# Pooled keys and values of the first two batches summed on TensorE in float32, their weights turned there, and a new decode of the layer weights

## The chip, the cores and the metric

The kernel runs on one core of one Trainium2 chip. The metric is device time in microseconds (us) of one execution, from three executions. "Span" is the time from the first to the last instruction of the profiled execution.

## What is computed

An attention with pooled keys and values feeds two layers, the first with a rational function inside, the second with a squared rectifier.

```python
def _attn_ref(q, k, v):                       # (8, 8, 576, 64) each, pool = 8
    k_p = k.reshape(B, H, Sp, pool, D).mean(axis=3)
    v_p = v.reshape(B, H, Sp, pool, D).mean(axis=3)
    scores = scale * np.matmul(q, k_p.transpose(0, 1, 3, 2))
    attn = np.exp(scores - np.max(scores, axis=-1, keepdims=True))
    attn = attn / (np.sum(attn, axis=-1, keepdims=True) + 1e-09)
    return np.matmul(attn, v_p)

def _moe_ref(x, w_in, w_out, a, b):           # x: 4608 x 512, w_in: 512 x 2048
    h = x @ w_in
    P = a[0] + a[1] * h + a[2] * h**2 + a[3] * h**3
    Q = 1.0 + np.abs(b[0]) * np.abs(h) + np.abs(b[1]) * h**2
    return (P / (Q + 1e-6)) @ w_out

def _moe2_ref(x, w_in, w_out):
    h = np.maximum(x @ w_in, 0.0)
    return h * h @ w_out
```

The weights are float64; q, k and v are float32, and q and k are large (some 33 times a tenth of a normal draw), so that the scores need the accuracy of float32.

## The kernel before

**Work and tiles.** The 4608 tokens are nine blocks of 512, and these stand in four groups (`SBS`: two, two, two and three blocks). Each group goes through four phases: phases 0 and 1 are the halves of the first layer's 2048 hidden columns, phases 2 and 3 those of the second. A phase is eight f-tiles of 128 columns for each block of the group; one f-tile of one block is a slot. The first group so has 64 slots, numbered 0 to 63; phases 0 and 1 are slots 0 to 31. A slot has `mm1` (12 matmuls of 128x512 into `h`), VectorE's and ScalarE's work on `h` (`first`, `second`), and `mm2` (12 matmuls into four `y` tiles). Both products take three passes over a high and a low float32r half. In phases 0 and 1 VectorE has six operations of 512 a slot, in 2 and 3 one.

**Attention.** A chunk is 128 tokens of all eight heads, four chunks a block. `qk` gives the scores, `row_max` and `exps` the exponentials, `norm` divides, `a_split` (L696) makes two fp16 tiles of 128 columns a head of them and has the DMA transpose them (`turn`, SP's queue), `av` (L711) multiplies with the split values, `x_out` makes the layer's input `x`. The first nine chunks (`NF`) take q and pooled k in float32, the others bf16 parts. Block 0 needs chunks 0 to 3, block 1 chunks 4 to 7; a batch is 4.5 chunks, so these use batches 0 and 1.

**Pooling.** Batch 0's k and v come in whole (`k_first`, `v_first`) and VectorE sums them over eight tokens; for all others the first of eight slices is loaded and seven are added to it by DMAs that POOL issues, one after the other (`k_add`, `v_add`). `v_split` makes three bf16 parts, with four small copies by DMA.

**Weights.** An f-tile's weights are 1 MB of float64 words. `w_raw` loads them into one of three buffers (`ya`, `yb`, `wraw`); `w_decode` (L486) takes the exponent on ScalarE (a copy scaled by 2^-112), moves the low word's bits (VectorE, or ScalarE in phase 1), joins them on VectorE (`stt`), joins the sign in a second `stt`, and makes the high and low halves. For the twelve f-tiles in `BY_DMA` (2 to 7 of phases 0 and 1) the second `stt` writes a tile `t` and frees the raw buffer; ScalarE writes the high half and the negated low one, and a DMA of POOL adds `t` to the latter. Each f-tile is then stored for the later groups.

**Order.** A planner (`Plan`) takes all instructions down with an estimate of their cost and gives out the program order of every engine by list schedules. SP and POOL issue DMAs in that order; some are tied to an instruction of another engine, so that they start no earlier than planned (`_holds`).

Of the kernel before, what the change touches and what calls it, by code (L numbers as in the profile page):

```python
# [34 lines left out]
LN_SHIFT = 60  # L35
A_SHIFT = 15
# [10 lines left out]
BY_DMA = {(ph, f) for ph in (0, 1) for f in range(2, FH)}  # L47


class View:  # L50
    """Part of a planned tile: what will be taken from the real one when it exists."""
# [28 lines left out]
    def apart(self, other):  # L80
        """Whether two views of a tile surely share nothing: where they part, they take slices
        of the same thing that do not meet."""
        for a, b in zip(self.chain, other.chain):
            if a == b:
                continue
            if a[0] != "__getitem__" or b[0] != "__getitem__":
                return False
            for i, j in zip(a[1][0], b[1][0]):
                (i0, i1), (j0, j1) = (
                    (x, x + 1) if isinstance(x, int) else (x.start or 0, x.stop or 1 << 30)  # L90
                    for x in (i, j)
                )
# [25 lines left out]
class Plan:  # L118
    """Takes down the kernel's instructions in the order of their meaning, with about what they
    take, and gives them out in an order that keeps the engines busy. The order comes from list  # L120
    schedules forwards (the most urgent of what is ready first) and backwards (as late as the
    engines allow, which is what says how urgent an instruction is)."""
# [249 lines left out]
def fused_kernel(  # L372
# [4 lines left out]
    kf: bass.AP,  # L377
# [77 lines left out]
    sh_bias = const.tile([128, 1], F32, "sh_bias")  # L455
    a_1 = const.tile([128, H, 128], F16, "a_1")
    a_2 = const.tile([128, H, 128], F16, "a_2")

    def setup():
# [3 lines left out]
        plan.add("dve", 0.07, [(fill, dict(out=a_2[:, :, KC:128], x=0.0))])  # L463

# [10 lines left out]
    def w_raw(ph, f, tag):  # L475
        """Words of an f-tile's part of w_in and of w_out."""
# [9 lines left out]
    def w_decode(ph, f):  # L486
        """2^-112 takes 7 * 128 off the exponent field of the high word seen as a float32:
        its 11 bits then hold a float32's exponent, 3 bits too low. On ScalarE, the low word's upper
        half u becomes its top 3 bits by rounding u / 8192 less almost a half."""
# [3 lines left out]
        act(n, AF.Copy, out=f32(g), in_=f32(g), scale=2.0 ** -112)  # L493
# [27 lines left out]
    xt = {}  # L521
    kst, vst, kp_t, vp_t = {}, {}, {}, {}
    q_in, q_t, e_t, sm_t, at_t, x_ps = {}, {}, {}, {}, {}, {}

    def k_add(b, r):
        if b == 1:
            shape, src = [128, H // 2, SP], kf[b, :, r].rearrange("p (g k) -> p g k", g=4)
        else:
            shape, src = [128, H, SP], kt[b - 2, :, r]
        n = 128 * shape[1] * SP * 4  # L530
        if r == 0:
            kp_t[b] = p1.tile(shape, F32, f"kp{min(b, 2)}")
# [4 lines left out]
    def v_add(b, r):  # L537
        n = SP * DM * 4
        if r == 0:
            vp_t[b] = p1.tile([SP, DM], F32, "vp")  # L540
            load(n, vp_t[b], vt[b, :, r], SUM_EARLY)
        else:
            load_add(n, vp_t[b], vt[b, :, r], SUM_EARLY)

    def k_first():
        """Batch 0's k, in room that the blocks' x takes later."""
        t = px.tile([128, 2, 4, TB], F32, "x").rearrange("p a b c -> p (a b c)")
        n = 4 * SP
        raw = t[:, 0:POOL * n].rearrange("p (r k) -> p r k", r=POOL)
        load(128 * POOL * n * 4, raw, kf[0])  # L550
        kp = t[:, POOL * n:(POOL + 1) * n].rearrange("p (g k) -> p g k", g=4)
        dve(
            POOL * n, "tensor_reduce",
            out=kp, in_=raw.rearrange("p r (g k) -> p g k r", g=4), axis=AX.X, op=ALU.add,
        )
        kp_t[0] = kp

    def v_first():
        t = px.tile([128, 2, 4, TB], F32, "x").rearrange("p a b c -> p (a b) c")[0:SP]
        load(SP * DM * POOL * 4, t, vt[0])  # L560
        vp_t[0] = p1.tile([SP, DM], F32, "vp")
        for i in range(2):
            d = slice(i * DM // 2, (i + 1) * DM // 2)
            dve(
                POOL * DM // 2, "tensor_reduce",
                out=vp_t[0][:, d], in_=t[:, :, d].rearrange("p r d -> p d r"), axis=AX.X, op=ALU.add,
            )

    def k_split(b):
# [3 lines left out]
        act(n, AF.Copy, out=k[0], in_=kp)  # L573
        tt(n, kp, kp, k[0], ALU.subtract)
# [19 lines left out]
    def q_first():  # L594
        """The first chunks' q, in room that weights take later."""
# [42 lines left out]
    def qk(c, half):  # L638
        """Scores of the even or of the odd heads: in what follows, head 2g + a is at a, g."""
# [3 lines left out]
        else:  # L643
            ps = ps_s.tile([128, H // 2, SP], F32, "sc")
# [18 lines left out]
        pe((0.95 if c < NF else 0.4) * len(list(runs(c))), mm)  # L663
        sc_t[c, half] = ps

    def row_max(c, half):
# [6 lines left out]
        dve(H // 2 * SP, "tensor_reduce", out=mx, in_=sc_t[c, half], axis=AX.X, op=ALU.max)  # L673
# [311 lines left out]
```

## Time and profile before

| | us |
|---|---|
| three executions | 1761.91, 1768.87, 1783.73 |
| their median | 1768.87 |
| span of the profiled execution | 1782.6 |
| that execution's own time | 1783.73 (the one of the three that can hold this span) |

The profiled execution is so the longest of the three, 14.9 us above the median. In it PE is busy for 94% of the span, DVE for 65%, ACT for 63%, POOL for 6%. A busy share is a mean over stages with different limits, so the first 420 us are read by stretches. "PE" are matmuls, "PEld" their weight loads, "SPq" SP's queue; an idle time in brackets names what ended it.

### The profile page before, as it was taken

The page shows a single profiled execution, that of the slowest core. Times are in us where ns is not written, and L with a number is a line of the kernel's source. Part 1 is how long each engine was busy: PE and PEld are TensorE (multiplying, and loading weights), DVE is VectorE, ACT ScalarE, POOL GpSimd, SP SyncE. Part 2 cuts the span into 40 slices and gives each one's busy share as a digit, 9 for nine tenths or more (in the row PEclk, how much of TensorE's full clock was granted, in tenths as well). Part 3 has the DMA queues.
Part 4 walks back from the last instruction along what each step waited for, and adds up shares of the span by engine and source line. Part 5 has one row for each costly group of instructions (what it writes and reads, how often), then busy time and mean ns, then how long its engine had stood idle before and what let it go on. Part 6 is the DMA issues. An engine that isn't in the chain of part 4 may idle for free.

```text
span 1782.6 us, 23502 instructions
## 1 busy us (share of the span) xinstructions
PE 1677.6 (94%) x8752; PEld 1369.3 (77%) x8752; DVE 1166.6 (65%) x1886; ACT 1129.2 (63%) x2336; POOL 98.2 (6%) x115
## 2 busy tenths in 40 slices
PE   2269899899999999999999999999999999999999
PEld 2148777687788888888888888888888888888887
DVE  7459999867569898344588994444988999211112
ACT  4467877678766666666666686766766666433332
POOL 1200011001000001010000110100000000000000
PEclk9989999999999999999999999999999999999999
DMA  9993757988690437493614395835402203103101
GB/s 255 181 102 119 225 139 240 288 235 222 201 322 24 166 73 229 85 263 85 212 36 177 73 225 130 212 113 172 119 12 108 82 1 118 71 1 138 51 24 48
DMA packets 126931, 248.62 MB, mean 139 GB/s; under 512 B 82904, under 2 KB 85080, under 8 KB 106008
## 3 DMA queue, kind: packets, MB, share of 16 engines
q1 hardware_dynamic: 113184, 219.12, 40.0%
q0 software_dynamic: 13632, 27.99, 10.3%
q8 instruction: 69, 1.13, 0.2%
q14 instruction: 46, 0.38, 0.1%
HBM read 176.69 MB, written 42.99 MB: 123 GB/s over the span
## 4 chain that ended last, share of the span: by engine, by line
PE 83%; DMA 10%; ACT 3%; DVE 2%; issue 1%; SPq 0%; POOL 0%; POOLq 0%; ACTq 0%; DVEq 0%
PE y L365 40%; PE h L365 40%; DMA vp<-vt 2%; DMA wraw<-wb 2%; PE xp L365 1%; PE sc L365 1%; DMA ya<-wb 1%; DMA wraw<-wa 1%; DMA at<-a 1%; DMA x<-vt 1%; ACT v L365 1%; DMA kp<-kf 1%; ACT w L365 1%; ACT wraw L365 1%; DMA w<-t 0%
## 5 line engine op out<-in xcount | busy, mean ns | idle before, releaser
L365 PE MATMUL h<-x,w 128*128 128x512 f32 x3456 | 838.6, 392 | 5.9 <-DVE p L365 5.4
L365 PEld LDWEIGHTS h<-x,w 128*128 128x128 f32 x3456 | 648.6, 189 | 144.2 <-DVE p L365 5.8
L365 PE MATMUL y<-g,w 128*128 128x512 f32 x1728 | 420.1, 391 | 10.1 <-DVE g L365 10.1
L365 PE MATMUL y<-w,g 128*128 128x512 f32 x1728 | 425.5, 395 | 4.0 <-DVE g L365 2.3
L365 PEld LDWEIGHTS y<-g,w 128*128 128x128 f32 x1728 | 324.1, 188 | 79.8 <-DVE g L365 12.4
L365 PEld LDWEIGHTS y<-w,g 128*128 128x128 f32 x1728 | 323.1, 189 | 72.9 <-DVE g L365 3.9
L365 ACT ACTIVATE s<-h 128x512 f32<-128x512 f32 x288 | 171.1, 594 | 282.8 <-PE h L365 274.3
L365 DVE TENSOR_TENSOR g<-w,g 128x512 fp32r<-128x512 f32 x144 | 99.4, 690 | 315.5 <-ACT g L365 308.2
L365 ACT ACTIVATE v<-s,ln_bias 128x512 f32<-128x512 f32 x144 | 104.4, 725 | 83.6 <-DVE s L365 82.2
L365 ACT ACTIVATE g<-s 128x512 fp32r<-128x512 f32 x144 | 91.0, 633 | 89.6 <-PE y L365 88.8
L365 ACT ACTIVATE p<-h,a_sb 128x512 f32<-128x512 f32 x144 | 111.8, 776 | 28.3 <-PE h L365 24.4
L365 DVE TENSOR_TENSOR p<-p,h 128x512 f32<-128x512 f32 x144 | 98.3, 683 | 31.0 <-ACT v L365 17.6
L365 DVE SCALAR_TENSOR_TENSOR g<-p,a_sb,v 128x512 fp32r<-128x512 f32 x144 | 107.7, 748 | 15.2 <-ACT v L365 13.6
L365 DVE SCALAR_TENSOR_TENSOR s<-s,b_abs,v 128x512 f32<-128x512 f32 x144 | 107.4, 746 | 9.8 <-ACT v L365 9.6
L365 DVE SCALAR_TENSOR_TENSOR w<-p,a_sb,w 128x512 f32<-128x512 f32 x144 | 107.4, 746 | 1.1
L365 DVE SCALAR_TENSOR_TENSOR p<-p,a_sb,h 128x512 f32<-128x512 f32 x144 | 106.7, 741 | 1.1 <-ACT s L365 0.6
L365 ACT ACTIVATE v<-v,ex_bias 128x512 f32<-128x512 f32 x144 | 104.0, 723 | 2.7
L365 ACT ACTIVATE v<-h,b_sb 128x512 f32<-128x512 f32 x144 | 99.1, 688 | 8.1 <-DVE p L365 4.9
L365 DVE SCALAR_TENSOR_TENSOR w<-s,g 128x512 f32<-128x512 f32 x144 | 99.1, 689 | 3.2
L365 DVE TENSOR_TENSOR g<-w,v 128x512 fp32r<-128x512 f32 x144 | 98.8, 686 | 1.9
L365 ACT ACTIVATE w<-s 128x512 f32<-128x512 f32 x144 | 90.9, 632 | 9.8 <-DVE g L365 5.9
L365 ACT ACTIVATE e<-sc,mx 128x72 f32<-128x72 f32 x256 | 78.5, 322 | 5.6 <-DVE mx L365 5.3
(86 smaller groups left out, 1120.9 us busy)
## 6 DMA issues: line engine op xcount, KB each, us to landing
w<-ws SPq DMA_DIRECT2D x96, 1024.0 KB
ws<-w SPq DMA_DIRECT2D x32, 1024.0 KB
q<-qt SPq DMA_DIRECT2D x27, 512.0 KB
kp<-kt POOLq DMA_DIRECT2D x42, 288.0 KB, 4.7
wraw<-wb SPq DMA_DIRECT2D x8, 1024.0 KB
wraw<-wa SPq DMA_DIRECT2D x7, 1024.0 KB
vp<-vt POOLq DMA_DIRECT2D x49, 144.0 KB, 5.5
yb<-wa SPq DMA_DIRECT2D x6, 1024.0 KB
```

What stands on the lines that cost most here:

```text
L365: made = fn(**{k: v.real() if isinstance(v, View) else v for k, v in kw.items()})
```

## The change

The order of the program changes nearly everywhere, since the planner's costs are new; these are the edits behind it.

- Batches 0 and 1 (`NK` = 2) no longer come pooled in slices. Their k and v are loaded as they stand, tokens on partitions (four tiles of 128 tokens and one of 64), and multiplied on TensorE in float32 with a 0/1 matrix `sums`, which POOL makes at the start with an identity `ident` (four `affine_select`). ScalarE copies the sums out of PSUM. `k_first`, `v_first`, `v_split` of batches 0 and 1 and the slices of batch 1 go.
- Chunks 0 to 8: the weights are transposed on TensorE in float32 (eight per chunk, into PSUM, VectorE and ScalarE copying one half each), and `av` is one float32 product a head in place of three fp16 ones. The DMA transposes of these chunks go. The values have M = 64, the transposes K = 128.
- `w_decode`: ScalarE's scaled copy becomes a leaky rectifier of slope -2^32, which sets bit 31 of negative words after the shift; the second `stt` goes for all 32 f-tiles, and the twelve of `BY_DMA` take VectorE's subtraction like the others, with no DMA.
- The score scale moves into k, and the row maximum is negated in the reduction (72 small operations go).
- The planner's costs: 2.72 us a product of 12 matmuls (2.592), 150 GB/s for an adding DMA (360), dearer transposes, and POOL in its backward pass.

```diff
     def w_decode(ph, f):
...
-        act(n, AF.Copy, out=f32(g), in_=f32(g), scale=2.0 ** -112)
+        act(n, AF.Prelu, out=f32(g), in_=f32(g), scale=2.0 ** -112, alpha=-(2.0 ** 32))
...
-        if (ph, f) in BY_DMA:
-            v = f32(p2.tile([128, 2, H, CH], BF16, "t").rearrange("p a h t -> p (a h t)"))
-            stt(n, v.bitcast(I32), g, -(2 ** 31), w, ALU.bitwise_and, ALU.bitwise_or)
-            act(n, AF.Copy, out=t[:, HI], in_=v)
-            act(n, AF.Copy, out=t[:, LO], in_=v, scale=-1.0)
-            load_add(WB / 2, f32(t[:, LO]), v)
-        else:
-            stt(n, w, g, -(2 ** 31), w, ALU.bitwise_and, ALU.bitwise_or)
-            act(n, AF.Copy, out=t[:, HI], in_=f32(w))
-            tt(n, t[:, LO], f32(w), f32(t[:, HI]), ALU.subtract)
+        act(n, AF.Copy, out=t[:, HI], in_=f32(w))
+        tt(n, t[:, LO], f32(w), f32(t[:, HI]), ALU.subtract)
...
+    def kv_first(b):
...
+        k, v = kv_t[2 * b:2 * b + 2]
+        for t, whole, rest in ((k, kn, km), (v, vn, vm)):
+            load(2 ** 20, t[:, 0:4], whole[b].rearrange("p (c n) -> p c n", c=4))
+            load(2 ** 17, t[0:S % 128, 4], rest[b])
...
+        parts = [(c, min(128, S - 128 * c)) for c in range(5)]
...
+        for c, n in parts:
+            m = n // POOL
+            for g in range(H // 2):
+                mm.append(dict(
+                    out=pk[:, g, 16 * c:16 * c + m], lhsT=k[0:n, c, g * 128:(g + 1) * 128],
+                    rhs=sums[0:n, S0W:S0W + m], start=True, stop=True,
+                ))
+        pe(2.2, mm)
...
+        act(H // 2 * SP, AF.Copy, out=kp_t[b], in_=pk, scale=SCALE)
...
+        for c, n in parts:
+            o = S0W - 16 * c
+            pe(0.9, [dict(
+                out=ps, lhsT=sums[0:n, o:o + SP], rhs=v[0:n, c], start=(c == 0), stop=(c == 4),
+            )])
...
+        act(DM, AF.Copy, out=vp_t[b], in_=ps)
...
-        dve(H // 2 * SP, "tensor_reduce", out=mx, in_=sc_t[c, half], axis=AX.X, op=ALU.max)
-        dve(0, "tensor_scalar", out=mx, in0=mx, scalar1=-1.0 / 64, scalar2=None, op0=ALU.mult)
+        dve(H // 2 * SP, "tensor_reduce", out=mx, in_=sc_t[c, half], axis=AX.X, op=ALU.max, negate=True)
...
+    def a_turn(c):
...
+            pe(0.3, [
+                dict(
+                    out=ps[:, i], lhsT=e[:, half * (H // 2) + i], rhs=ident,
+                    start=True, stop=True, is_transpose=True,
+                ) for i in range(H // 2)
+            ])
+            o = t[:, half * (H // 2):(half + 1) * (H // 2)]
+            if half == 0:
+                dve(TB, "tensor_copy", out=o, in_=ps)
+            else:
+                act(TB, AF.Copy, out=o, in_=ps)
...
-        at(t + 5, "t", a_split, c)
+        at(t + 5, "t", a_turn if c < NF else a_split, c)
...
-    k_first()
-    q_first()
+    kv_first(0)
     load_consts()
-    v_first()
-    at(-S0 + 3, "t", v_split, 0)
+    at(-S0 + 6, "t", kv_first, 1)
```

SP's queue near its start, before the change: the parts of v (`v_...`), the first of v's slices of batch 1 (`vp<-vt`), raw weights (`ya`, `yb`), and the transposes of chunk 0 (`at<-a`).

```order
L365 DMA q<-qf 128x512
L365 DMA v_167<-v_167 56x512
L365 DMA v_188<-v_167 16x512
L365 DMA v_179<-v_179 56x512
L365 DMA vp<-vt 72x512
L365 DMA v_188<-v_179 16x512
L365 DMA ya<-wa 128x2048
L365 DMA a_sb<-ca 128x4
L365 DMA_TRANSPOSE at_242<-a_228 128x8x128
L365 DMA_TRANSPOSE at_256<-a_90 128x8x128
L365 DMA yb<-wa 128x2048
```

The same place after: batch 1's k and v (`kn`, `km`, `vn`, `vm`) between the raw weights of f-tiles 3 to 6 (`ya`, `yb`, `wraw`, `ya`).

```order
L368 DMA x<-kn 128x2048
L368 DMA x<-km 64x512
L368 DMA w<-qf 128x512
L368 DMA ya<-wa 128x2048
L368 DMA q<-qf 128x512
L368 DMA x<-vn 128x2048
L368 DMA yb<-wa 128x2048
L368 DMA wraw<-wa 128x2048
L368 DMA q<-qf 128x512
L368 DMA x<-vm 64x512
L368 DMA a_sb<-ca 128x4
L368 DMA ya<-wa 128x2048
```

The transposes and the copies of v have left SP's queue; the loads that take their place are a megabyte each, and the next row there is f-tile 7 (`yb<-wa`).

PE around the first `mm1`, before: the end of chunk 3's product, scores of chunk 5 around the first `mm1`s, and the first rows of chunk 4's product, which needs the transposed tile `at_573`.

```order
L365 MATMUL xp<-at_506,v_188 64x128
L365 MATMUL sc<-kp_92,q 128x72 x4
L365 MATMUL h<-x,w 128x512 x12
L365 MATMUL sc<-kp_92,q 128x72 x4
L365 MATMUL h<-x,w 128x512 x24
L365 LDWEIGHTS v_167
L365 MATMUL xp<-at_573,v_167 64x64
```

The same place after: sums of batch 1's v (`h<-x,sums`), transposes (`y_...<-ident,e`, `sc<-ident,e`), products of chunks 2 and 3 (`xp<-t,x`), and scores of chunks 4 to 6.

```order
L368 MATMUL h<-x,sums 72x512 x2
L368 MATMUL sc<-x,q 64x72 x8
L368 MATMUL xp<-t,x 64x128 x8
L368 MATMUL h<-x,sums 72x512
L368 MATMUL y_433<-ident,e 72x128 x4
L368 MATMUL y_440<-ident,e 72x128 x4
L368 MATMUL sc<-x,q 128x72 x4
L368 MATMUL h<-x,sums 72x512 x2
L368 MATMUL xp<-t,x 64x128 x8
L368 MATMUL sc<-x,q 128x72 x4
L368 MATMUL h<-x,w 128x512 x12
L368 MATMUL sc<-ident,e 72x128 x4
```

The five sums of batch 1's v and chunk 3's transposes now stand on PE ahead of the first `mm1`.

VectorE in the first chunks, before: chunk 1's normalization (`e<-e,sm`), its two fp16 tiles (`a_...`), and f-tile 2's two `stt` (to `wraw` and `t`).

```order
L365 TENSOR_SCALAR wraw<-wraw 128x1024
L365 TENSOR_TENSOR e<-e,sm 128x576
L365 SCALAR_TENSOR_TENSOR wraw<-wraw 128x1024
L365 TENSOR_SCALAR ya<-ya 128x1024
L365 TENSOR_TENSOR a_228<-e,a_228 128x8x56
L365 TENSOR_TENSOR a_90<-e,a_228 128x8x16
L365 COPY a_90<-a_228 128x8x72
L365 COPY a_90<-a_90 128x8x16
L365 SCALAR_TENSOR_TENSOR t<-wraw 128x1024
```

The same place after: copies of the transposed weights (`t<-y_...`), one `stt` an f-tile, and its low half (`w<-yb,w`, `w<-wraw,w`).

```order
L368 COPY t<-y_212 72x512
L368 RECIPROCAL sm<-sm 128x8
L368 SCALAR_TENSOR_TENSOR yb<-yb 128x1024
L368 TENSOR_TENSOR e<-e,sm 128x576
L368 TENSOR_REDUCE mx<-y_230 128x4
L368 SCALAR_TENSOR_TENSOR wraw<-wraw 128x1024
L368 TENSOR_TENSOR w<-yb,w 128x1024
L368 COPY t<-y_271 72x512
L368 TENSOR_REDUCE mx<-y_278 128x4
L368 SCALAR_TENSOR_TENSOR x<-xp,x 128x4x128
L368 TENSOR_TENSOR w<-wraw,w 128x1024
```

For f-tile 2 VectorE still has a shift and two long operations, but the raw buffer is now held until the last of them.

## Rows read from the trace of the kernel before

**Rows 1.** The page: busy time by engine; PE's tenths in 40 slices.

```profile
PE 1677.6 (94%) x8752; PEld 1369.3 (77%) x8752; DVE 1166.6 (65%) x1886; ACT 1129.2 (63%) x2336; POOL 98.2 (6%) x115
PE   2269899899999999999999999999999999999999
```

**Rows 2.** Stretches of the span: length, busy us (instructions), granted clock, DMA share, GB/s.

```profile
0.00:20.00 20.00, 5.15 (x32) 4.95 (x34) 10.52 (x11) 4.78 (x11) 2.11 (x6) 1.00 0.89 284
20.00:60.00 40.00, 11.02 (x100) 9.56 (x98) 32.08 (x63) 24.28 (x75) 10.37 (x11) 1.00 1.01 235
60.00:99.40 39.40, 10.36 (x88) 9.06 (x88) 15.02 (x29) 18.59 (x54) 5.75 (x7) 1.00 1.18 150
99.40:124.20 24.80, 15.04 (x93) 11.38 (x93) 11.65 (x23) 14.33 (x37) 0.86 (x1) 0.83 1.10 98
124.20:320.00 195.80, 184.50 (x866) 148.70 (x863) 176.92 (x270) 151.19 (x256) 17.53 (x20) 0.99 0.62 180
320.00:420.00 100.00, 93.36 (x468) 74.23 (x467) 76.69 (x108) 74.42 (x152) 7.83 (x9) 0.95 0.90 266
420.00:1782.60 1362.60, 1358.14 (x7118) 1111.38 (x7116) 843.75 (x1389) 841.64 (x1757) 53.71 (x62) 1.00 0.41 120
```

**Rows 3.** The chain that ended last: start us, us, what.

```profile
2.61 14.49 DMA x<-vt
...
51.68 15.46 DMA at<-a
67.59 10.74 DMA vp<-vt
79.02 16.63 DMA vp<-vt
96.30 11.79 DMA vp<-vt
114.40 8.45 DMA v<-v
...
141.00 2.72 PE h L365 x12
...
203.49 9.27 DMA wraw<-wa
...
245.72 8.65 DMA w<-t
```

**Rows 4.** PE in order of time: start us, us, instructions, idle before.

```profile
69.86 1.98 PE L365 MATMUL sc<-kp,q 64*128 64x72 f32 x8 [1.40 <-ACT e L365]
...
93.59 0.42 PE L365 MATMUL xp<-at,v 128*64 128x128 f16 x4 [16.49 <-DMA at<-a]
...
99.53 4.28 PE L365 MATMUL h<-x,w 128*128 128x512 f32 x12
103.75 1.11 PE L365 MATMUL sc<-kp,q 64*128 64x72 f32 x8
```

**Rows 5.** DVE in order of time: first work on slot 0, last on slot 31.

```profile
109.84 0.75 DVE L365 SCALAR_TENSOR_TENSOR s<-s,b_abs,v 128x512 f32<-128x512 f32 x1
...
316.61 0.69 DVE L365 TENSOR_TENSOR g<-w,v 128x512 fp32r<-128x512 f32 x1
```

**Rows 6.** Groups of instructions: count, busy us, mean ns of one, idle before.

```profile
L365 DVE SCALAR_TENSOR_TENSOR wraw<-wraw 128x1024 int32<-128x1024 int32 x24 | 29.3, 1220 | 2.7 <-ACT wraw L365 2.6
...
L365 ACT ACTIVATE w<-t 128x1024 fp32r<-128x1024 f32 x24 | 24.9, 1061 | 0.5 <-DVE t L365 0.4
...
L365 ACT ACTIVATE wraw<-wraw 128x1024 f32<-128x1024 f32 x15 | 17.5, 1169 | 11.6 <-DMA wraw<-wb 8.7 <-DMA wraw<-wa 2.9
...
L365 DVE TENSOR_SCALAR mx<-mx 128x4 f32<-128x4 f32 x72 | 12.0, 169 | 1.3
...
L365 DVE TENSOR_TENSOR w<-wraw,w 128x1024 fp32r<-128x1024 f32 x9 | 11.0, 1222 | 3.3 <-ACT w L365 3.3
```

**Rows 7.** DMA packets of the first 140 us.

```profile
DMA packets 20023, 24.24 MB, mean 173 GB/s; under 512 B 14856, under 2 KB 16168, under 8 KB 18536
```

More of the change, by code (lines that the diff above doesn't have):

```diff
@@ L35 @@
 LN_SHIFT = 60
+SCALE = 1.0 / POOL / 8
 A_SHIFT = 15
@@ L292, in _backward @@
         at = {op: 0.0 for op in self.ops}
-        waiting, ready = [], {q: [] for q in ("pe", "act", "dve", "dma")}
+        waiting, ready = [], {q: [] for q in ("pe", "act", "dve", "pool", "dma")}
         free, done, ends, now = dict.fromkeys(ready, 0.0), {}, [], 0.0
@@ L455, in fused_kernel @@
     sh_bias = const.tile([128, 1], F32, "sh_bias")
+    ident = const.tile([128, 128], F32, "ident")
+    sums = const.tile([128, WS], F32, "sums")
     a_1 = const.tile([128, H, 128], F16, "a_1")
@@ L463, in setup @@
         plan.add("dve", 0.07, [(fill, dict(out=a_2[:, :, KC:128], x=0.0))])
+        masks = (
+            (sums, 1, -POOL, S0W * POOL), (sums, -1, POOL, POOL - 1 - S0W * POOL),
+            (ident, 1, -1, 0), (ident, -1, 1, 0),
+        )
+        for t in (sums, ident):
+            plan.add("dve", 0.2, [(fill, dict(out=t, x=1.0))])
+        for t, p, n, base in masks:
+            pool(
+                0.5, nc.gpsimd.affine_select, out=t, in_=t, pattern=[[n, t.shape[1]]], base=base,
+                channel_multiplier=p, compare_op=ALU.is_ge, fill=0.0,
+            )
     def load_consts():
@@ L540, in v_add @@
             vp_t[b] = p1.tile([SP, DM], F32, "vp")
-            load(n, vp_t[b], vt[b, :, r], SUM_EARLY)
+            load(n, vp_t[b], vt[b - NK, :, r], SUM_EARLY)
         else:
[L543 to L567, printed above, removed]
+            load_add(n, vp_t[b], vt[b - NK, :, r], SUM_EARLY)
@@ new lines, in kv_first @@
+    def kv_first(b):
+        if b == 0:
+            for _ in range(2 * NK):
+                kv_t.append(px.tile([128, 2, 4, TB], F32, "x").rearrange("p a b c -> p (a b) c"))
+        k, v = kv_t[2 * b:2 * b + 2]
+        for t, whole, rest in ((k, kn, km), (v, vn, vm)):
+            load(2 ** 20, t[:, 0:4], whole[b].rearrange("p (c n) -> p c n", c=4))
+            load(2 ** 17, t[0:S % 128, 4], rest[b])
+            if t is k and b == 0:
+                q_first()
+        parts = [(c, min(128, S - 128 * c)) for c in range(5)]
+        ps = ps_h.tile([128, TB], F32, "h")
+        pk = ps[:, 0:H // 2 * SP].rearrange("p (g k) -> p g k", g=H // 2)
+        mm = []
+        for c, n in parts:
[6 more added lines that the diff above has]
+        pe(2.2, mm)
+        kp_t[b] = kv_t[2][:, 5 + b, 0:H // 2 * SP].rearrange("p (g k) -> p g k", g=H // 2)
+        act(H // 2 * SP, AF.Copy, out=kp_t[b], in_=pk, scale=SCALE)
+        ps = ps_h.tile([128, TB], F32, "h")[0:SP]
+        for c, n in parts:
[3 more added lines that the diff above has]
+            )])
+        vp_t[b] = kv_t[3][0:SP, 5 + b]
+        act(DM, AF.Copy, out=vp_t[b], in_=ps)
@@ L694, in norm @@
                 act(SP, AF.Copy, out=e[:, h], in_=e[:, h], scale=sm[:, h:h + 1])
+    def a_turn(c):
+        e = e_t.pop(c)[2]
+        t = f32(p2.tile([128, 2, H, CH], BF16, "t").rearrange("p a h t -> p (a h t)"))
+        t = t[0:SP].rearrange("p (h t) -> p h t", h=H)
+        for half in range(2):
+            if c < CPB:
+                ps = ps_y.tile([128, TB], F32, f"y{2 * (c % 2) + half}")[0:SP]
+            elif half == 0:
+                ps = ps_s.tile([128, TB], F32, "sc")[0:SP]
+            else:
+                ps = ps_x.tile([128, TB], F32, "xp")[0:SP]
+            ps = ps.rearrange("p (h t) -> p h t", t=CH)
+            pe(0.3, [
[7 more added lines that the diff above has]
+                dve(TB, "tensor_copy", out=o, in_=ps)
+            else:
+                act(TB, AF.Copy, out=o, in_=ps)
+        at_t[c] = t
     def a_split(c):
@@ L712, in av @@
         q_t.pop(c)
+        ps = ps_x.tile([128, TB], F32, "xp").rearrange("p (g t) -> p g t", t=CH)
+        mm = []
+        if c < NF:
+            t = at_t.pop(c)
+            for g in range(H // 2):
+                for o, n, b in runs(c):
+                    for par in range(2):
+                        h = 2 * g + par
+                        mm.append(dict(
+                            out=ps[64 * par:64 * par + 64, g, o:o + n],
+                            lhsT=vp_t[b][:, h * D:(h + 1) * D], rhs=t[:, 4 * par + g, o:o + n],
+                            start=True, stop=True,
+                        ))
+            pe(1.3, mm)
+            x_ps[c] = ps
+            return
         t1, t2 = at_t.pop(c)
-        ps = ps_x.tile([128, H // 2, CH], F32, "xp")
-        mm = []
         for g in range(H // 2):
@@ L899, in fused_kernel @@
     need = [-S0 + 3] + [starts[b * S // CH] for b in range(1, B)]
-    for b in range(1, B):
+    for b in range(NK, B):
         place_batch(b, need[b], max(need[b - 1], need[b] - 24))
```

60 lines of the change are left out of this document (33 added, 27 removed).

## The prediction

> **What bounds the kernel now.** I read the page first: PE is busy for 94% of the span and, of 40 slices, only the first three, and a little the fifth and the eighth, are not full [rows 1]. So the question is what holds PE back in the first quarter, and I cut the span into stretches [rows 2]. The reader is to see three things there. From 420 us to the end PE is busy for 1358.1 of 1362.6 us; one `mm1` of twelve matmuls takes 2.72 us [rows 3], and no edit of this change takes work off PE in it. That stretch stays. From 0 to 99.4 us PE is busy for 26.5 us (5.15 + 11.02 + 10.36) and does none of the layers' work. From 99.4 to 420 it works on the layers, with 9.8 us of idle time up to 124.2, 11.3 up to 320 and 6.6 up to 420.
>
> The chain of waits says what the first 120 us are made of [rows 3]: the load of batch 0's v (14.49 us), a DMA transpose (15.46), three adding DMAs of batch 1's v (10.74, 16.63, 11.79), and the small copies of v's parts (8.45). PE's own list shows one of these from the other side: chunk 3's product waits 16.49 us for its transposed tile, and the first `mm1` starts at 99.53 [rows 4]. VectorE has slot 0 at 109.84 and is done with slot 31 at 317.30 [rows 5]: 207.5 us for 32 slots, in which PE needs 32 x 5.44 = 174.1. There VectorE is busy for 176.9 of 195.8 us and PE for 184.5 [rows 2]: two engines near their end at once.
>
> While DMA is "busy" for over 100% between 20 and 124 us it moves 235, then 150, then 98 GB/s, against 284 in the first 20 us [rows 2]. 14856 of the 20023 packets of that time are under 512 B [rows 7]. So the start is bound by slow kinds of transfer, and by their order, not by bytes.
>
> **The change, part by part.** *The start.* Every piece of the chain named above goes for batches 0 and 1: no slices, no adding DMA, no transpose, no copies of v. What replaces them is loads of whole rows. I count in SP's order what must land before VectorE can touch slot 0: in its program order slot 0 stands behind f-tile 7's first operations, so it needs eight raw tiles (8 x 1.05 MB), k and v of both batches (4 x 1.18 MB) and six q tiles (6 x 0.26 MB), 14.7 MB together. At the 284 GB/s of the first stretch, the nearest row, since it holds the same kind of load, that is 52 us. With 1 us before the first issue, two VectorE operations on the last tile (at most 1.22 us each [rows 6]) and 2 us for loads that wait until a raw buffer is free, slot 0 comes at 57 us. Faster loads help little: VectorE's own instructions ahead of slot 0 add up to 39 us by their groups' means, and from the landing of the first raw tile, at about 8 us, they end at 47. At the 235 GB/s of 20 to 60 us it is 68.
>
> PE has to fit its new work in front of that. In float32 eight score matmuls of 72 columns take 1.98 us at 69.86 and 1.11 at 103.75 [rows 4], 0.25 or 0.14 us each. By columns a transpose or a value product of 128 is 0.44 or 0.25 us, a sum of v (512) 1.76 or 0.99; a sum of k (16 columns) I put at a score matmul. Before the first `mm1` stand 40 sums of k, 10 of v, 44 scores, 32 transposes and 32 products: 37 us at the faster rate, 66 at the slower. From the landing of k, at about 6 us, that ends at 43 or 72. I take the faster for most of it, since PE is then busy for over half the time, and so the loads are the bound.
>
> *Slots 0 to 31.* VectorE has the same work there within 4 us: it loses the fp16 tiles and small operations (0.169 us each [rows 6]) of chunks 4 to 7 and the second `stt` of two f-tiles, and gains f-tiles 6 and 7, which were decoded ahead of slot 0 before. For the twelve f-tiles a subtraction of 1.222 takes the place of an `stt` of 1.220 [rows 6]: nothing. ScalarE loses one copy of 1.061 for each, 12.7 us. The leaky rectifier is in no row; the nearest is the copy it replaces, 1.169 for 1024 columns, and I bound it by that copy from below and by twice it from above; it costs nothing while ScalarE has room (151 of 195.8 us busy). So I keep the 207.5 us, take off the 8.45 us of the v copies, which fell behind slot 0, and add 3 us for float32 in chunks 4 to 7. Its bounds are 0 (heads in pairs, as the fp16 products ran) and four chunks x 6 us = 24, of which PE's idle 21.1 us can hide most. Slot 31 is then done at 57 + 202 = 259 instead of 317.3: 58.3 us earlier.
>
> The adding DMA of 8.65 us on the chain at 245.72 [rows 3] goes too; VectorE's 1.22 us stands for it. On the other side the raw buffer is free only after that subtraction, so the next raw load (9.27 us on the chain at 203.49) starts later. I let these two cancel.
>
> *Slots 32 to 63.* Sixteen f-tiles lose an `stt`, 19.5 us of VectorE, which is busy for 76.7 of 100 us there. PE's idle 6.6 us bounds the gain; I take 2. Chunk 8's float32 is within that.
>
> *After 420:* 0, with 3 us to either side for the new order.
>
> The sum is made on the profiled execution: 1783.7 - 58.3 - 2 = 1723.4, so 1723 us. That execution lies 14.9 us above the median of its three. Where this spread comes from the trace doesn't show; the start, with its irregular DMA waits, is the likeliest place, and then the new kernel has less of it. Against the median 1723 is 2.6% faster.
>
> [...] The granted clock was 0.83 between 99.4 and 124.2 us, with PE busy for 15.0 of 24.8 [rows 2], and the first `mm1` took 4.28 us [rows 4] instead of 2.72. [...] No row of this trace has a transpose on PE. [...]
>
> **The rivals.** *Float32 at the lower clock.* PE's 66 us stand between k's landing and the first `mm1`, at 72 us; with 4.28 us for it slot 0 comes at 76, 19 later than in the sum: 1742. With 3 us more from chunks 4 to 7, 1745. For it: eight scores in 1.98 us at 69.86 [rows 4]. Against it: PE was idle for three quarters of that time and will not be.
>
> *The raw buffers are the bound.* A buffer's round in phase 1 is now a load (9.27), the rectifier and the shift on ScalarE (1.17 each), the `stt` (1.22), the high half (1.06) and the subtraction (1.22): 15.1 us without waits, and each of the five has to wait for its turn among a slot's work. With two buffers and an f-tile every two slots (10.9 us) the limit is a round of 21.8 us. At 27 us, six f-tiles lose 5 us each: 30 us, 1753. For it: the stalls after 200 us are raw loads on the chain [rows 3]. Against it: the f-tiles outside the twelve were held as long before.
>
> *The loads are slow, and the kernel with them.* All of the start now hangs on one queue of 14.7 MB. If it moves as between 99.4 and 124.2, 98 GB/s [rows 2], slot 0 comes at 153 us instead of 109.84 and the kernel takes some 1783.7 + 43 - 10 = 1817. It decides from below 136 GB/s, where slot 0 is no earlier than before. For it: 40 us at 150 and 25 at 98 GB/s. Against it: those packets were small ones of transposes and adding DMAs, which go.
>
> **How the numbers follow.** The forecast has 0.74; the lower clock 0.12; the raw buffers 0.08; the slow loads 0.06. Within the forecast slot 0 lies between 50 and 64 us, the 32 slots between 192 and 210, and the later stalls may give up to 5 more: 1783.7 - 83 to 1783.7 - 44, 1701 to 1740. The range reaches a little below that, since the median may keep part of its 14.9 us, and up to the two cases around 1750: 1695 to 1751. About 2% (35 us, so 1733.5) is what a measurement can tell from no change: of the forecast some 0.72 lies below that, the rest of it with the two middle cases makes 0.22, and slower has 0.06.
>
> **What would show it.** Right: the first `mm1` at 45 to 58 us and VectorE's slot 0 at 50 to 64; over 270 GB/s up to there, with few small packets; slot 31 done at 245 to 272; no DMA of k, v or `at` on the chain before slot 0; PE full from some 360 us on. The lower clock shows as transposes and products of over 0.4 us apiece and a first `mm1` near 72. The raw buffers show as PE waiting for loads of `wraw` or for `w` between 130 and 260 us. Wrong altogether: slot 0 after 100 us, or stalls of over 10 us beyond 420, which I have put at zero.

## The result, and the profile after

| | before | after |
|---|---|---|
| median | 1772.60 us (4 executions) | 1719.52 us (4 executions, 1717.20 to 1722.30) |
| after / before | | 0.9683, interval 0.9633 to 0.9733 |
| profiled execution, span | 1783.73, 1782.6 | 1717.20, 1715.5 |

The changed kernel is faster by 3.2%; 1723.0 was forecast. Over 50 further executions the kernel before scatters from 1750.6 to 1793.8 us, the changed one over eight by 5.4 us. The ratios leave before's highest times out. Experiments on the changed kernel are therefore judged against its own 1717 to 1722.

The page after, the rows that answer to [rows 1]:

```profile
PE 1694.9 (99%) x8844; PEld 1382.5 (81%) x8844; DVE 1119.3 (65%) x1762; ACT 1115.2 (65%) x2324; POOL 75.8 (4%) x93
...
PE   8999999999999999999999999999999999999998
```

The stretches after, to [rows 2] (length, busy us of PE, PEld, DVE, ACT and POOL with instructions, granted clock, DMA share, GB/s). The first four are cut as there, the others at slot 31's end and 106 us later:

```profile
0.00:20.00 20.00, 13.63 (x65) 12.00 (x66) 4.10 (x11) 4.39 (x7) 1.25 (x8) 1.00 0.79 301
20.00:60.00 40.00, 39.45 (x257) 28.01 (x257) 28.59 (x49) 31.18 (x119) 0.00 (x0) 0.87 0.60 215
60.00:99.40 39.40, 38.99 (x248) 31.37 (x248) 36.29 (x61) 38.79 (x105) 0.00 (x0) 1.00 0.12 43
99.40:124.20 24.80, 24.80 (x122) 20.26 (x121) 24.52 (x36) 20.06 (x32) 0.00 (x0) 1.00 0.58 212
124.20:255.00 130.80, 125.75 (x552) 102.11 (x551) 124.16 (x180) 103.46 (x156) 11.47 (x13) 1.00 0.63 188
255.00:360.00 105.00, 102.31 (x537) 83.13 (x536) 71.60 (x100) 84.11 (x167) 12.18 (x14) 1.00 0.94 274
360.00:1715.50 1355.50, 1350.00 (x7075) 1105.60 (x7073) 830.05 (x1330) 833.26 (x1745) 50.87 (x58) 1.00 0.41 120
```

PE is nearly full from its first instruction on, at 6.4 us, and the DMA share in 20 to 60 us is 0.60 instead of 1.01.

The clock of 1.00 in the first row above, and up to 99 us in [rows 2], is not a reading. The traces hold no clock ahead of their first record, which is 1.00 from 25.8 us on here and from 102.3 us on before, and the view prints 1.00 where it has none. The records of both hold two levels, 1.00 and 0.50. What PE's rows took tells the level: a sum of v (two records) at 15 and at 49 us in this kernel, then in e7, a run below, at 23 us, where the clock on record is 0.50.

```profile
15.09 1.98 PE L368 MATMUL h<-x,sums 128*72 128x512 f32 x2
...
49.44 1.08 PE L368 MATMUL h<-x,sums 128*72 128x512 f32 x2
```

```profile
22.91 1.98 PE L368 MATMUL h<-x,sums 128*72 128x512 f32 x2
```

So PE's rows here go by the lower level, 0.50, up to 25.8 us, and again from 36.0 to 46.3 us, which is on record. That is 29.7 of the 50.7 us from its first instruction to the first `mm1`.

Packets of the first 140 us are 4714 instead of 20023 [rows 7]:

```profile
DMA packets 4714, 24.25 MB, mean 173 GB/s; under 512 B 800, under 2 KB 800, under 8 KB 2080
```

VectorE's first work on slot 0 and its last on slot 31, to [rows 5]:

```profile
63.73 0.74 DVE L368 SCALAR_TENSOR_TENSOR s<-s,b_abs,v 128x512 f32<-128x512 f32 x1
...
253.38 0.69 DVE L368 TENSOR_TENSOR g<-w,v 128x512 fp32r<-128x512 f32 x1
```

So the span cuts into three terms, here for each kernel's profiled execution (slot 0 starts; slots 0 to 31; the rest), beside the median of all its executions. All later readings start from this table. Two things limit them. A profiled execution can lie off its kernel's median (before 11.1 us above it, e4 6.1, e1 5.2; e6 4.5 below, e2 3.4). And every kernel is planned anew, so a term also holds what the new order of the program does.

| kernel | first `mm1` | slot 0 | slots 0–31 | rest | median |
|---|---|---|---|---|---|
| before | 99.5 | 109.8 | 207.5 | 1465.3 | 1772.6 |
| forecast | 45–58 | 57 | 202 | – | 1723.0 |
| after | 57.1 | 63.7 | 190.3 | 1461.4 | 1719.5 |
| after, once more | 56.8 | 63.4 | 188.5 | 1463.9 | 1718.0 |
| start only (e1) | 66.1 | 73.7 | 216.2 | 1464.9 | 1751.4 |
| decode only (e2) | 69.0 | 75.9 | 196.0 | 1469.7 | 1746.8 |
| costs only (e3) | 86.0 | 96.6 | 196.7 | 1470.0 | 1764.0 |
| all but the costs (e4) | 65.1 | 72.0 | 199.5 | 1456.8 | 1723.8 |
| second `stt` kept (e9) | 59.5 | 66.6 | 203.8 | 1467.2 | 1738.9 |
| adding DMAs kept (e10) | 57.3 | 63.1 | 197.6 | 1460.8 | 1723.9 |
| sums in one bf16 pass (e5) | 49.7 | 56.3 | 188.6 | 1461.3 | 1711.2 |
| SP without ties (e6) | 57.5 | 63.9 | 189.3 | 1462.4 | 1721.8 |
| PE busy early (e7) | 63.1 | 68.6 | 191.9 | 1464.2 | 1724.7 |
| DMA transposes kept (e8) | 82.2 | 91.4 | 186.1 | 1458.5 | 1738.1 |
| wide sums of k (e12) | 59.3 | 66.0 | 191.3 | 1463.6 | 1722.6 |

### The profile page after: what moved, and what is told of

It is laid out like the page before. It is cut to its first block, busy times and chain, and to the rows that moved or that the text cites. A ratio compares the mean times of both kernels' runs of the same rounds, so it can differ in the third digit from the quotient of the medians.

```text
span 1715.5 us, 23452 instructions
## 1 busy us (share of the span) xinstructions
PE 1694.9 (99%) x8844; PEld 1382.5 (81%) x8844; DVE 1119.3 (65%) x1762; ACT 1115.2 (65%) x2324; POOL 75.8 (4%) x93
## 4 chain that ended last, share of the span: by engine, by line
PE 88%; DVE 5%; DMA 3%; ACT 2%; issue 1%; DVEq 0%; ACTq 0%; POOLq 0%
PE h L368 43%; PE y L368 42%; PE sc L368 2%; PE xp L368 2%; DVE w L368 2%; DMA kp<-kt 1%; DVE p L368 1%; DVE g L368 1%; ACT e L368 1%; DVE s L368 1%; ACT w L368 1%; DMA ws<-w 0%; DMA ya<-wb 0%; DMA yb<-wa 0%; DMA wraw<-wa 0%
```

## Experiments: which part brought it

**The changed kernel once more (a2)**, on the chip of e7 and e8:

> The changed kernel once more, beside the two others, so that they are compared on one chip: 1717 to 1722 us, the first mm1 within 1 us of 57.1 and slot 0 within 1 us of 63.7.

1717.95 us (1716.91 to 1720.84; ratio 0.9694, 0.9653 to 0.9736): that is how well it repeats.

**The start alone (e1).** The changed kernel, new costs included, with the decode of before, its second `stt` and its twelve adding DMAs:

```diff
-        act(n, AF.Prelu, out=f32(g), in_=f32(g), scale=2.0 ** -112, alpha=-(2.0 ** 32))
+        act(n, AF.Copy, out=f32(g), in_=f32(g), scale=2.0 ** -112)
...
+        if (ph, f) in BY_DMA:
+            v = f32(p2.tile([128, 2, H, CH], BF16, "t").rearrange("p a h t -> p (a h t)"))
+            stt(n, v.bitcast(I32), g, -(2 ** 31), w, ALU.bitwise_and, ALU.bitwise_or)
```

> The changed kernel with the old decode of the weights (scaled copy, sign by a second stt, twelve f-tiles by an adding DMA). Theory (the start gives nearly all): VectorE's slot 0 within 5 us of the changed kernel's 63.7, slot 31 done some 10 to 17 us later than its 254.1, time 1728 to 1738. Rival (the decode gives a good half, since the DMAs of the old one also fill the start): slot 0 after 75 us and a time over 1745.

1751.38 us (ten executions, 1746.34 to 1756.60; ratio 0.9928, interval 0.9882 to 0.9974). The theory of the prediction falls: slot 0 comes 36 us earlier than before, but the 32 slots then take 216 us. The rival's time comes true, its slot 0 after 75 us just not. Slot 0, at 73.7, is 10 us behind that of after, and the first adding DMA is issued later still, so it is not these DMAs that hold it back here:

```profile
75.18 1.05 POOL L369 DMA_DIRECT2D w<-t  x1 [72.99 <-ACT w L369]
```

**The decode alone (e2).** The kernel before with the rectifier, one `stt` and the subtraction for all:

> The kernel before with the new decode alone (leaky rectifier, VectorE's subtraction for all f-tiles). Theory: its start still waits for adding DMAs and transposes, so slot 0 stays after 95 us; the stalls from 200 to 320 us shrink; time 5 to 17 us under the kernel before. Rival (the twelve adding DMAs of 512 KB are what crowds the queue in the start): slot 0 before 85 us and 25 us or more gained.

1746.76 us (1742.83 to 1751.55; ratio 0.9898, 0.9851 to 0.9945). With the slices and DMA transposes of the start all still there, slot 0 comes 34 us earlier, as the rival said. The transposes from 0 to 120 us, before and then in this kernel (count, and ns min/median/max for which the issue of one held SP's queue; the one at 51.68 us held it for 9.9 us and landed after 15.46 [rows 3]):

```profile
L365 SPq DMA_TRANSPOSE at<-a x10: 1240/2150/14925, 32.5 to 98.9; - x10
...
  PE xp L365: 40.8, 10
```

```profile
L365 SPq DMA_TRANSPOSE at<-a x16: 1231/1320/4952, 31.8 to 118.6; - x16
...
  PE xp L365: 20.2, 8
```

The second row of each says how long products waited for transposed tiles (us, times). Without the adding DMAs of decoded weights the longest transpose falls from 14.9 to 5.0 us. That these DMAs made it long is not shown, since the next run, e3, keeps them all and comes as low, here from 0 to 140 us:

```profile
L365 SPq DMA_TRANSPOSE at<-a x16: 1232/1702/5060, 31.3 to 132.3; - x16
...
  PE xp L365: 15.3, 5
```

The slices of batch 1's v land after 10.7 us in the median before, 5.4 in this kernel and 4.6 in e3. The run parts the decode from the start, but neither the DMAs from the `stt` that goes with them nor either from the new order.

**The planner's costs alone (e3).** The kernel before with the new costs:

```diff
-        plan.add("pool", 1.05, [call], n / 360e3, early)
+        plan.add("pool", 1.05, [call], n / 150e3, early)
...
-        pe(2.592, [
+        pe(2.72, [
```

> The kernel before with the planner's new costs alone. Theory: within 10 us of the kernel before either way. Rival (the new costs are what straightens the order): 20 us or more gained.

1763.95 us (1758.18 to 1767.36; ratio 1.0007, 0.9968 to 1.0047). In the profile slot 0 is 13 us earlier and the slots 11 us shorter; by the ratio nothing is measured. Against before's median of that chip, 1779.29, it would be 15 us; which of the two it is stays open behind before's spread. So with every transfer of the start still there, another order, or an execution other than before's slowest of four, moves the terms by over 10 us.

**All but the costs (e4).** The reverse edit in the changed kernel (POOL stays in the backward pass):

> The changed kernel with the planner's old costs (2.592 us a product, 360 GB/s for adding DMAs, old attention and transpose costs). Theory: 1715 to 1728, the work is the same and PE stays full after 360 us. Rival: 1735 or more, with stalls after 250 us.

1723.82 us (1721.42 to 1729.95; ratio 0.979, 0.9698 to 0.9881): the new costs are worth some 4 us beside the rest. Its profile is of its slowest execution, so the three terms exaggerate.

## Experiments: what in the decode was worth it

**The second `stt` kept (e9).** No adding DMA, but the sign set as before for all 32 f-tiles:

```diff
-        act(n, AF.Prelu, out=f32(g), in_=f32(g), scale=2.0 ** -112, alpha=-(2.0 ** 32))
+        act(n, AF.Copy, out=f32(g), in_=f32(g), scale=2.0 ** -112)
...
+        stt(n, w, g, -(2 ** 31), w, ALU.bitwise_and, ALU.bitwise_or)
```

> The changed kernel with the sign by a second stt and a plain scaled copy, without the adding DMAs. New theory (the adding DMAs of the old decode cost some 30 us: their landing and the tile they hold): within 10 us of the changed kernel, slot 31 done by 264 us. Rival (VectorE's second stt was the cost): over 1738 and slot 31 after 275.

1738.89 us (1733.82 to 1740.79; ratio 0.9799, 0.9768 to 0.9831), 19.4 above after: the rival's time, with slot 31 done at 270.4 and not after its 275. Slots 0 to 31, first after, then here:

```profile
63.70:254.10 190.40, 185.22 (x898) 150.44 (x897) 182.06 (x270) 157.72 (x279) 11.12 (x13) 1.00 0.51 158
```

```profile
67.00:270.40 203.40, 192.42 (x930) 155.22 (x929) 198.38 (x292) 164.31 (x307) 11.43 (x13) 0.98 0.49 150
```

VectorE is given 16.3 us more and the stretch grows by 13.0: in after it is busy for 96% of it, so there is little idle time in which more work could hide. Sixteen further `stt` fall behind slot 31, where the rest grows by 5.8 us.

**The adding DMAs kept (e10).** The rectifier and one `stt`, but for the twelve f-tiles the way over `t` and POOL's DMA in place of the subtraction:

```diff
-        stt(n, w, g, 3, w, ALU.logical_shift_left, ALU.bitwise_or)
...
+        if (ph, f) in BY_DMA:
+            v = f32(p2.tile([128, 2, H, CH], BF16, "t").rearrange("p a h t -> p (a h t)"))
+            stt(n, v.bitcast(I32), g, 3, w, ALU.logical_shift_left, ALU.bitwise_or)
```

> The changed kernel with the leaky rectifier, but with the twelve adding DMAs: the one stt writes the tile that the DMA adds. Theory (adding DMAs): 1742 to 1756, slot 0 after 68 us and slot 31 after 275, as with the whole old decode. Rival (the stt): 1715 to 1730.

1723.86 us (1723.31 to 1726.18; ratio 0.9721, 0.9693 to 0.975), 4.3 above after, as the rival said:

```profile
63.10:260.70 197.60, 188.10 (x885) 151.31 (x883) 181.83 (x267) 169.79 (x281) 20.58 (x23) 0.97 0.72 210
```

VectorE has the same 182 us to do, and the stretch is 7 us longer: it idles 15.8 us instead of 8.3. The two alone come to 23.7 us; the old decode in full (e1) costs 31.9. The other 8 us appear only with both; in e1's stretch VectorE is busy for 199.8 us and idle for 16.4:

```profile
73.70:289.90 216.20, 199.44 (x926) 158.68 (x925) 199.82 (x293) 177.78 (x316) 24.49 (x28) 0.95 0.68 197
```

The old costs alone move the changed kernel's median by as much as e10 does (e4, 4.3 us), so the DMAs' share is not told apart from that of another order; the `stt`'s 19.4 us stand clear of it.

## Experiments: what bounds the new start

PE in order of time up to the first `mm1`, after; a float32 matmul stands as two records (a batch's twenty sums of k as x40), a transpose as one (a chunk's eight as x8):

```profile
6.37 8.78 PE L368 MATMUL h<-sums,x 128*128 128x16 f32 x40 [6.37 <-DMA x<-kn]
15.09 1.98 PE L368 MATMUL h<-x,sums 128*72 128x512 f32 x2
17.00 4.76 PE L368 MATMUL y<-x,w 64*128 64x72 f32 x32
21.69 4.81 PE L368 MATMUL h<-x,sums 128*72 128x512 f32 x6
26.34 0.60 PE L368 MATMUL y<-ident,e 128*72 128x128 f32 x4
...
29.48 1.09 PE L368 MATMUL xp<-t,x 72*64 72x128 f32 x16
30.50 1.07 PE L368 MATMUL y<-ident,e 128*72 128x128 f32 x8
...
32.54 5.66 PE L368 MATMUL h<-sums,x 128*128 128x16 f32 x40
...
51.81 1.11 PE L368 MATMUL sc<-x,q 64*128 64x72 f32 x8 [0.42 <-ACT e L368]
...
57.11 3.32 PE L368 MATMUL h<-x,w 128*128 128x512 f32 x12
```

From k's landing to the first `mm1` PE stands still for 0.5 us, 0.42 of it in the one wait shown. The chain of waits is PE's own up to 45.9 us; from there to the first `mm1` it is mostly ScalarE's work on the chunks.

**Sums in one bf16 pass (e5).** The upper 16 bits of k and v are summed, the low bits left out; the rest is unchanged:

```diff
-                    out=pk[:, g, 16 * c:16 * c + m], lhsT=k[0:n, c, g * 128:(g + 1) * 128],
-                    rhs=sums[0:n, S0W:S0W + m], start=True, stop=True,
+                    out=pk[:, g, 16 * c:16 * c + m], lhsT=top(k[0:n, c, g * 128:(g + 1) * 128]),
+                    rhs=sums_b[0:n, S0W:S0W + m], start=True, stop=True,
```

> The changed kernel with the sums of k and v taken on the upper 16 bits of each word (bf16 views, one pass): it leaves the lower bits of k and v of batches 0 and 1 out. Theory (PE's new work bounds the start): sums of k in under 3 us a batch where they took 8.8 and 5.7, first mm1 at 40 to 50 us instead of 57.1, time 5 to 13 us less. Rival (the loads bound the start, as predicted): first mm1 still after 54 us.

1711.18 us (1707.94 to 1713.91; ratio 0.9647, 0.9615 to 0.9679), and the first `mm1` 7.4 us earlier. PE's order there:

```profile
6.02 0.85 PE L368 MATMUL h<-sums_b,x 128*128 128x16 bf16 x20 [6.02 <-DMA x<-kn]
11.79 0.58 PE L368 MATMUL h<-x,sums_b 128*72 128x512 bf16 x1 [4.91 <-DMA x<-vn]
...
26.24 1.92 PE L368 MATMUL y<-ident,e 128*72 128x128 f32 x8
...
30.01 0.79 PE L368 MATMUL h<-sums_b,x 128*128 128x16 bf16 x20
```

The sums of k shrink from 14.4 to 1.6 us, but PE then waits 4.91 us for v: the loads stand some 5 us behind PE as the bound. The clock takes another part of what the sums save: its first rise on record is at 44.7 us here, and eight transposes at 26.24 us take 1.92 us, against 1.07 at 30.50 in after.

**SP's ties in the start dropped (e6).** Loads planned before 60 us start as soon as SP reaches them:

```diff
-            if op in self.holds:
+            if op in self.holds and not (op.queue == "sp" and self.start[op] < 60.0):
```

> The changed kernel without the planner's ties on SP's loads of the start, so that each is issued as early as its buffer allows. Rival (loads bound the start): slot 0 at least 4 us before 63.7 and the time 3 us or more below the changed kernel. Theory (PE and the order bound it): slot 0 within 2 us, time within 3 us.

1721.78 us (1716.74 to 1726.61; ratio 0.9715, 0.9672 to 0.9759). Its first 20 us, to the first row of the stretches after:

```profile
0.00:20.00 20.00, 13.88 (x67) 12.26 (x68) 4.37 (x11) 4.62 (x9) 1.24 (x8) 1.00 0.91 347
```

347 GB/s instead of 301, and slot 0 comes at 63.9: more bytes sooner brought nothing here.

**PE busy from 2 us on (e7).** Ten float32 matmuls of `ident` with itself ahead of batch 0's sums:

```diff
+        if b == 0:
+            pe(2.0, [
+                dict(out=ps[:, 0:128], lhsT=ident, rhs=ident, start=True, stop=True) for _ in range(10)
+            ])
```

> The changed kernel with ten float32 matmuls of the identity with itself ahead of batch 0's sums of k; their result is never read. Theory (PE is the bound of the start, and part of what it costs there is the lower clock it starts at): PE is busy from about 3 us, batch 0's forty records of k's sums take under 6.5 us instead of 8.78 and the first sums of v about 1.1 instead of 1.98, the first mm1 comes 3 to 6 us before 57.1, and the kernel takes 1713 to 1717. Rival (the start waits for the landing of v and of q, and for the exponentials, as soon as PE's sums are shorter): k's sums are as much shorter, but the first mm1 is within 1.5 us of 57.1 and the time within 2 us of 1719.5.

1724.73 us (1723.85 to 1726.47; ratio 0.9728, 0.9679 to 0.9778): both miss. The sums of k took 5.73 us as expected, PE then waited 5.04 for v, and the first `mm1` came 6 us later, not earlier. The clock rose at 6.9 us instead of 25.8, but fell at 10.3 and again at 37.6, and PE had the lower level for 42.5 of the 61.1 us from its first instruction to the first `mm1`.

**Wide sums of k (e12).** k is summed as v is, 512 columns a matmul, and turned by four transposes a batch:

```diff
-                    out=pk[:, g, 16 * c:16 * c + m], lhsT=k[0:n, c, g * 128:(g + 1) * 128],
-                    rhs=sums[0:n, S0W:S0W + m], start=True, stop=True,
...
+                out=ps, lhsT=sums[0:n, o:o + SP], rhs=k[0:n, c], start=(c == 0), stop=(c == 4),
...
+            out=pk[:, g], lhsT=kt[:, g * 128:(g + 1) * 128], rhs=ident[0:SP, 0:SP],
+            start=True, stop=True, is_transpose=True,
```

> The changed kernel with k summed as v is: the 0/1 matrix is the stationary operand and k's 512 columns stream (five matmuls a batch instead of twenty of 16 columns), and the 72x512 sums are then turned on TensorE in four transposes a batch into the layout that the scores need. The result is the same. Theory (the clock falls at 35 to 45 us behind batch 1's sums of 16 columns, each with a weight load of its own and hardly a column to stream; with wide products it stays up): the granted clock is over 0.9 in each stretch of 5 us from 30 to 55 us, sums and turn of batch 1 take under 6.5 us, the first mm1 comes 3 to 6 us before 57.1, and the kernel takes 1713 to 1717. Rival (the clock falls for what the whole start is, sparse in columns, not for these sums): the granted clock still is at 0.5 to 0.6 for 5 us or more between 30 and 55 us, the first mm1 is within 2 us of 57.1 or later, and the time 1718 to 1726.

1722.55 us (1720.33 to 1725.18; ratio 0.9708, 0.9674 to 0.9743). PE by stretches of 5 us (busy, granted clock, DMA share, GB/s) in after, e7 and e12:

```profile
30.00:35.00 5.00, 5.00 (x50) 1.00 0.94 385
35.00:40.00 5.00, 5.00 (x33) 0.60 1.01 413
40.00:45.00 5.00, 5.00 (x43) 0.50 0.35 131
45.00:50.00 5.00, 5.00 (x42) 0.87 0.10 27
```

```profile
20.00:25.00 5.00, 5.00 (x25) 0.50 0.92 289
...
30.00:35.00 5.00, 5.00 (x38) 0.92 0.42 159
...
40.00:45.00 5.00, 5.00 (x30) 0.50 0.69 239
```

```profile
20.00:25.00 5.00, 5.00 (x15) 0.50 0.80 272
...
30.00:35.00 5.00, 5.00 (x14) 0.61 0.43 172
35.00:40.00 5.00, 5.00 (x40) 1.00 0.43 123
```

In e12 the clock stays up behind batch 1's sums, as its theory wants, but stands at 0.50, the lower of the two levels on record, from 20 to 30 us, and at 0.61 and 0.54 in 30 to 35 and 60 to 65. The last of these is at the first `mm1`. So the narrow sums are not needed for the clock to fall: here it falls at 16.9 us (0.69 in 15 to 20), and no sum of 16 columns is in the kernel. The first `mm1` (59.3) and the time are those of the rival; its clock, at 0.5 to 0.6 for 5 us behind 30 us, comes true as little as the theory's 0.9. In all three kernels PE was busy for the whole of the stretches shown. What decides where the clock falls stays open.

**DMA transposes kept (e8).** The changed kernel with fp16 tiles, DMA transposes and fp16 products for chunks 0 to 8, v split after TensorE's sums:

```diff
-        at(t + 5, "t", a_turn if c < NF else a_split, c)
+        at(t + 5, "t", a_split, c)
```

> The changed kernel with the weights of chunks 0 to 8 as before: two fp16 tiles, transposed by DMA, three fp16 products a head, and v of batches 0 and 1 split in parts after TensorE's sums. Theory (with the adding DMAs and the slices gone, the DMA transposes are what is left of the slow start; their 15 us each come from sharing the queues with raw loads of a megabyte): slot 0 comes 10 us or more after 63.7, a transpose in the first 60 us takes over 8 us, and the kernel takes 1728 to 1745. Rival (the transposes were slow only beside the adding DMAs; PE gives back in transposes and float32 products what the DMAs cost): slot 0 within 5 us of 63.7, a transpose under 5 us, and the time within 5 us of 1719.5.

1738.05 us (1737.62 to 1741.62; ratio 0.981, 0.9767 to 0.9852). The theory's time and slot 0 (91.4) come true, its reason doesn't:

```profile
L368 SPq DMA_TRANSPOSE at<-a x15: 1231/1264/2567, 40.2 to 118.5; - x15
...
  PE xp L368: 6.2, 4
```

```profile
60.00:100.00 40.00, 26.01 (x193) 21.11 (x194) 31.32 (x57) 35.30 (x106) 0.00 (x0) 0.65 0.71 202
```

No transpose holds the queue for over 2.6 us and the products wait 6.2 us in all. PE is busy for 26.0 of 40 us and has a clock of 0.65 there. The chain of waits from 51 to 82 us has ScalarE's and VectorE's work on `e`, `a`, `v` and the raw tiles where it had transposes before; this part was read from the chain and not tried by itself.

## Why the prediction was right, and where not

**The time and the stage.** Nearly the whole gain lies ahead of slot 32, as forecast: 46.1 + 17.2 of the 67.1 us between the spans; the rest gives 3.9, for 2 ± 3 forecast. PE is nearly full from 60 us on. The median lies 3.5 us below the forecast and in its range. That it lies so near is in part luck: slot 0 came 6.7 us later than forecast and the 32 slots took 11.7 us less, and the sum starts at before's execution of 1783.7 us; from the median 1772.6 the same 60.3 us would have given 1712. Two of the signs failed, as PE and not the loads was the bound: the load of k stands on the chain (PE's first row waits for it), and the rate up to slot 0 stayed below 270 GB/s (301, then 215 in the stretches). None of the rivals became the kernel as a whole.

**"The start is bound by slow kinds of transfer."** Held in part. Either half of the change brings slot 0 forward: start alone 36.1 us, decode alone 33.9, both together 46.1, and the costs alone 13.2. The step that failed is the attribution: I gave all 52.8 us to the start's edits and nothing to the decode, six of whose adding DMAs are issued in the first 110 us. That a slice or a transpose was slow for the crowd of these DMAs fits e2, but e3 has both nearly as fast or faster with the DMAs still there; crowd, order and before's slow execution are not told apart.

**"Slot 0 comes at 57 us" and "the loads are the bound".** It came at 63.7, PE is the bound (e5, e6), and the loads are 5 us behind it. The failed step is the pricing of PE. I read "x8" in [rows 4] as eight matmuls; it is four of two records each, while a transpose is one. Up to the first `mm1`, by the sums of the timeline's rows: sums of k 14.4 us (5.6 to 10 priced), scores 14.0 (6.2 to 11, from 44 matmuls that are 56), sums of v 13.2 (9.9 to 17.6), transposes 5.3 (8 to 14), products 5.3 (8 to 14). The total of some 52 lies between my 37 and 66, since the misses by kind go both ways. "I take the faster for most of it, since PE is then busy" was the wrong choice: PE was busy for all but 0.5 us and still had the lower level for 29.7 of the 50.7 us. So the lower clock, which I made a rival, is there for a good half of PE's time, and the first `mm1` came 15 us before that rival's 72. Its sign, transposes and products of over 0.4 us apiece, could not show: at the lower level eight transposes took 1.92 us and eight products (16 records) 1.97 (after, at 43.92 and 42.02 us, granted clock 0.50).

**"207.5 us kept for the slots."** The premise held: VectorE has 182.1 us of work there, before 183.9 of 207.5 us:

```profile
109.80:317.30 207.50, 188.49 (x909) 151.65 (x909) 183.92 (x284) 157.73 (x272) 16.66 (x19) 0.97 0.64 171
```

What went was its idle time, 23.6 us down to 8.3, and I had taken 5.5 off the stretch, not 17.2. "I let these two cancel" is the failed step as far as the runs tell: with the subtraction for the adding DMA the stretch is 7 us shorter (e10), which another order can also bring. The raw buffers, which it holds longer, do show: three raw loads (6.85, 5.43 and 8.18 us) stand on after's chain in slots 0 to 31, but PE idles for 5.2 us there in all. Float32 in chunks 4 to 7, 3 us, is not seen apart.

**"A subtraction takes the place of an `stt`: nothing."** Right in the sum of VectorE (e10 has 181.8 us, after 182.1). But the sign by the rectifier is what makes that exchange possible: without it VectorE has 16 us more (e9) and the kernel 19.4. The prediction priced what left and what came, and not what the subtraction would have cost without the rectifier; so it said little about what each edit of the decode is worth.

**The rectifier** costs what the copy did (first row 1162 ns against 1169 [rows 6]); the lower bound was the value:

```profile
L368 ACT ACTIVATE wraw<-wraw 128x1024 f32<-128x1024 f32 x15 | 17.4, 1162 | 6.9 <-DMA wraw<-wb 4.5 <-DMA wraw<-wa 2.3
...
L368 DVE TENSOR_TENSOR w<-wraw,w 128x1024 fp32r<-128x1024 f32 x15 | 18.3, 1219 | 1.7 <-ACT w L368 1.6
```

**Transposes and the clock.** The rival of the lower clock had the first `mm1` near 72. It came at 57.1: the granted clock is back at 0.87 in 45 to 50 us, among transposes, products and sums. It had risen at 25.8 us, ahead of the first transpose (26.34), and fallen to 0.50 at 36.0, behind sixteen of them; in e12 it fell at 16.9 us behind four. What the transposes do to the clock is not shown: no run changes them alone.

**The spread.** That the irregular start makes before's spread, and that the new kernel has less of it, fits: 43 us over 50 executions, 5.4 over eight. But on the chip where before scatters by 43 us over 25, the kernels with one part changed have little spread too: 10.3 us over ten executions in e1, 8.7 in e2 and 9.2 in e3, and e3 has every transfer of the old start. So these transfers alone don't make it; what does stays open.

## What to carry to other kernels

Don't add the gains of two edits that relieve the same start: alone they brought slot 0 forward by 36.1 and 33.9 us, together by 46.1. Take one kind of transfer away before pricing the others at what they took, and run a new order of the program by itself, since it is part of every edit here. Where two engines are both near their end in a stretch, price each edit by the engine's busy and idle time in that stretch, since little idle time is left there to take up a longer one: in e9 16.3 us more of VectorE's work made such a stretch 13.0 us longer. Before multiplying by a count of records, find out how many records an instruction has. Where a view gives the full clock, compare it with what equal rows take.

## What was not expected

- Busy early was not quicker: ten spare matmuls from 2 us on made the first sums 3 us shorter and left the clock at 0.50 from 15 to 30 and from 40 to 50 us, and the first `mm1` 6 us later (e7).
- In after the granted clock fell to 0.60 and 0.50 between 35 and 45 us with PE busy for all of the 10 us; the sums of k take 8.78 us at the lower level, and 5.66 where the first 3.5 us of them are at the full one.
- A sum of k with 16 columns takes 0.28 to 0.44 us (5.66 and 8.78 over twenty), about as much as a float32 score of 72 columns (0.28 to 0.50: 1.11 and, in [rows 4], 1.98 over four); its weight loads are busy for nearly all of it, 10.7 of 10.8 us (the records of 128 rows, matmuls and then loads):

```profile
L368 PE MATMUL h<-sums,x 128*128 128x16 f32 x64 | 10.8, 320 | 6.4 <-DMA x<-kn 6.4
...
L368 PEld LDWEIGHTS h<-sums,x 128*128 128x128 f32 x64 | 10.7, 263 | 6.4 <-issue 6.3
```

- A float32 transpose on TensorE takes 0.13 us at the full clock (1.07 over eight, at 30.50 us in after), half of the 0.25 us that I had priced at the full clock.
